# Early K features with the maximum as ScalarE's bias, joined signs, paired sums and a narrower w_out product

## The chip, the cores and the metric

One core of a Trainium2 chip runs the whole kernel. The metric is the device time of one execution in microseconds (us). Names of the engines in the profile: PE is TensorE's matmuls, PEld its weight loads, DVE is VectorE, ACT is ScalarE, POOL is GpSimd, SP the engine that issues all DMAs.

## The reference

```python
proj = x @ w_phi; proj -= max(abs(proj), axis=-1)             # attention features, q and k
phi(x) = concat([exp(proj), exp(-proj)])                      # 256 features per row
kv = phi(k).T @ v;  z = sum_s phi(k)
attn = (phi(q) @ kv) / (phi(q) @ z + 1e-6)                    # B, H, S, D = 8, 8, 576, 64
h = x @ w_in;  g = max(h, 0) + alpha * min(h, 0);  y = g @ w_out     # 4608 tokens, 512 -> 2048 -> 512
logits = y @ phi                                              # soft mixture, 32 slots
slot_in = softmax(logits, over tokens).T @ y;  slot_out = experts(slot_in)
out = softmax(logits, over slots) @ slot_out
```

The weights `w_in` and `w_out` come as 64-bit floats and are converted on the chip.

## The kernel before, in words

`attention_prelu_softmoe` is one program, written as steps. `at(slot, phase, fn)` puts pieces of work into a table of steps, and the loop at its end runs the steps from -45 to 195. A scheduler then sets each engine's own order, from the priorities of this order and from its estimates of durations; each engine runs its instructions in that order, so one that waits holds up all behind it.

- **K pairs** (`k_pair`, 32 of them, two heads each). `project` multiplies K by `w_phi` into the two banks of the one buffer `pk` (pool `ps_b`, shared with the q projections `pq`). `feature` calls `features` for each head: VectorE takes the absolute maximum of 4 x 128 values (L281), subtracts it (L283), and ScalarE writes exp(x) and exp(-x) with one instruction of 512 each (L286, L287). `project_tail` and `feature_tail` do the same for the last 64 rows of two pairs at once. `kv` multiplies the features with V on TensorE (L336) and counts them: pairs 0 to 7 with matmuls on ones (L344), later ones from sums that VectorE makes in `total` (L322, L324), `total_tail` (L328). ScalarE copies the result (L352), `turn` transposes it, and `keep` copies it twice on VectorE (L365, L366). Fourteen pairs come early, the others one per six steps.
- **Weight converts** (`conv`, 16 pieces of `w_in`, then 16 of `w_out`). `first` splits 512 doubles: Abs and Sign on ScalarE (L197, L198), a clamp, a shift, a mask and a scaled product of the low word on VectorE (L199 to L202), a second Abs (L203). `second` adds (L207) and multiplies by the sign (L209). A `w_in` piece is then split in high and low (L222, L223). A `w_out` piece is transposed (L236) and multiplied by `phi`: four matmuls into four groups of 32 rows (L243), a copy (L245), a matmul that adds the groups (L249) and a copy on VectorE (L250).
- **Q pairs** (`q_pair`): the projection (L407), the maximum over partitions on GpSimd (L419, `partition_all_reduce`), the subtraction (L423), two exps (L429), the products with kv and z (L440, L445). For block 0 all of it lies ahead of the first step; `q_finish` takes the reciprocal of the denominator (L462, L463), sends it through DRAM (L465, L470), multiplies (L486) and splits into `xhi`, `xlo` (L479, L480).
- **The first layer** (`gemm`, 12 blocks of 384 tokens, 16 steps each): 12 matmuls per step (L520) into one of two banks `ph`, ScalarE's Relu (L527), VectorE's leaky part (L528). Every step of a block needs `xhi` and `xlo` of the whole block; step c of block 0 needs piece c of `w_in`.

## Time and profile before

| | |
|---|---|
| time, median of 3 runs | 974.15 us (971.86 to 974.99) |
| the profiled execution | 973.75 us, span of its instructions 971.9 us |
| PE busy | 928.3 us, 96% of the span |
| DVE busy | 722.1 us, 74% |
| ACT busy | 443.6 us, 46% |
| POOL busy | 143.5 us, 15% |
| PE busy in 40 slices, tenths | 6888989999989999999999999999999999899997 |
| DVE busy in 40 slices, tenths | 6998999989686687677678778677757767864233 |
| ACT busy in 40 slices, tenths | 5876757766635345245335344353342341221113 |

One slice is 24.3 us. Where PE reads 9 the core is at work on matmuls nearly all the time; the slices below that are the first four, two around 275 us, and the end. In the views, "idle before" is the time an engine stood still ahead of a group of instructions, and "<-" names what it waited for.

### The profile page before, as it was taken

What the parts mean: (1) busy time and instruction counts of PE and PEld (TensorE: products, weight loads), DVE (VectorE), ACT (ScalarE), POOL (GpSimd) and SP (SyncE); (2) the same over time, 40 slices, a digit from 0 to 9 for tenths busy, and PEclk for the clock granted to TensorE, in tenths of its full rate; (3) what the DMA queues carried; (4) which work ended last, traced back from release to release, by engine and by line L of the source; (5) the groups of instructions that cost most, each with busy time, mean ns of one, the idle gap of its engine ahead of it and who ended that gap; (6) DMA issues with size and microseconds to landing.
All of it is one profiled execution on the core that took longest, in us unless ns stands there. A gap on an engine that the chain in (4) does not pass through costs nothing.

```text
span 971.9 us, 20072 instructions
## 1 busy us (share of the span) xinstructions
PE 928.3 (96%) x8178; PEld 654.1 (67%) x8178; DVE 722.1 (74%) x1425; ACT 443.6 (46%) x867; POOL 143.5 (15%) x84
## 2 busy tenths in 40 slices
PE   6888989999989999999999999999999999899997
PEld 3446676777668676676677776776777667786454
DVE  6998999989686687677677778677756767864233
ACT  5876757766635345245335344353342341221113
POOL 4102212112112112122022112121130220000000
PEclk9898999999999999999999999999999999999999
DMA  7345655674231031031211210200212609478999
GB/s 272 119 141 177 207 169 196 213 203 122 64 87 28 23 85 43 26 78 53 51 44 42 59 53 25 75 26 23 54 34 72 177 1 302 159 268 260 311 354 335
DMA packets 75675, 122.22 MB, mean 126 GB/s; under 512 B 7872, under 2 KB 49472, under 8 KB 75584
## 3 DMA queue, kind: packets, MB, share of 16 engines
q1 hardware_dynamic: 75584, 120.95, 40.3%
q8 instruction: 64, 1.05, 0.5%
q14 instruction: 27, 0.22, 0.1%
HBM read 99.82 MB, written 21.10 MB: 124 GB/s over the span
## 4 chain that ended last, share of the span: by engine, by line
PE 74%; DVE 17%; DMA 4%; issue 2%; ACT 2%; SPq 0%; DVEq 0%; ACTq 0%
PE ph L520 37%; PE num L440 5%; PE pkv L336 5%; PE pS L625 4%; PE pl L556 4%; PE pq L407 3%; PE den L445 3%; PE pk L293 2%; PE pso L866 2%; DVE m L207 2%; DVE gT L528 1%; PE pe L846 1%; DVE mx L281 1%; PE po L902 1%; DVE rest L202 1%
## 5 line engine op out<-in xcount | busy, mean ns | idle before, releaser
L520 PE MATMUL ph<-xhi,w 128*128 128x384 f32 x1536 | 430.8, 351 | 8.2 <-ACT xhi L479 4.0
L520 PEld LDWEIGHTS ph<-xhi,w 128*128 128x128 f32 x1536 | 280.3, 189 | 71.5 <-issue 38.0
L520 PE MATMUL ph<-xlo,w 128*128 128x384 f32 x768 | 257.9, 341 | 0.9 <-DVE xlo L480 0.8
L419 POOL PARTITION_ALL_REDUCE mb<-pj x48 | 137.4, 2864 | 477.4 <-ACT pj L413 326.8
L527 ACT ACTIVATE gT<-ph 128x384 f32<-128x384 f32 x192 | 93.3, 488 | 245.3 <-PE ph L520 239.9
L528 DVE SCALAR_TENSOR_TENSOR gT<-gT,alpha_rest,ph 128x384 f32<-128x384 f32 x192 | 115.7, 604 | 103.8 <-ACT gT L527 102.4
L520 PEld LDWEIGHTS ph<-xlo,w 128*128 128x128 f32 x768 | 144.4, 189 | 9.7 <-issue 4.8
L547 DVE STREAM_TRANSPOSE gb<-gT 128x384 f32<-128x384 f32 x162 | 92.0, 571 | 2.9
L429 ACT ACTIVATE qe<-pj 128x768 f32<-128x768 f32 x90 | 72.2, 839 | 22.9 <-DVE pj L423 14.0
L440 PE MATMUL num<-qe,kv 128*64 128x192 f32 (+1 forms) x488 | 68.6, 411 | 3.5 <-ACT qe L429 3.3
L336 PE MATMUL pkv<-kall 128*64 128x256 f32 x464 | 57.9, 393 | 1.3 <-ACT kall L287 0.7
L281 DVE TENSOR_REDUCE mx<-pk 128x4 f32<-128x512 f32 (+1 forms) x80 | 49.5, 623 | 7.2 <-PE pk L293 5.8
L407 PE MATMUL pq<-qraw,wp 64*128 64x384 f32 x192 | 46.8, 545 | 7.9 <-DMA qraw<-in_qT_dram 4.1
L286 ACT ACTIVATE kall<-kall 128x512 f32<-128x512 f32 x60 | 37.5, 627 | 30.4 <-DVE kall L283 30.2
L440 PEld LDWEIGHTS num<-qe,kv 128*64 128x64 f32 x488 | 31.1, 136 | 27.8 <-issue 18.0
L324 DVE TENSOR_TENSOR ks<-ks,kall 128x256 f32<-128x256 f32 x96 | 47.4, 517 | 0.4
L336 PEld LDWEIGHTS pkv<-kall 128*64 128x64 f32 x464 | 31.6, 140 | 23.5 <-issue 4.8
L423 DVE TENSOR_TENSOR pj<-pj,mb 128x768 f32<-128x768 f32 x48 | 44.8, 932 | 0.0
L283 DVE TENSOR_TENSOR kall<-pk,mx 128x512 f32<-128x512 f32 x60 | 40.8, 680 | 2.2 <-PE pkv L336 1.7
L293 PE MATMUL pk<-wp,kall 64*128 64x128 f32 x512 | 39.5, 293 | 2.9 <-issue 2.6
L293 PEld LDWEIGHTS pk<-wp,kall 64*128 64x128 f32 x512 | 32.9, 194 | 12.8 <-issue 10.8
L413 ACT COPY pj<-pq 128x768 f32<-128x768 f32 x44 | 35.0, 796 | 13.4 <-PE pq L407 13.2
(203 smaller groups left out, 1157.6 us busy)
## 6 DMA issues: line engine op xcount, KB each, us to landing
w<-in_w_dram SPq DMA_DIRECT2D x46, 256.0 KB
kall<-in_v_dram SPq DMA_DIRECT2D x30, 320.0 KB
qraw<-in_qT_dram SPq DMA_DIRECT2D x48, 192.0 KB
bc<-rc_d SPq DMA_DIRECT2D x24, 384.0 KB
out_dram<-os SPq DMA_DIRECT2D x18, 512.0 KB
raw<-in_w_in_dram SPq DMA_DIRECT2D x16, 512.0 KB
raw<-in_w_out_dram SPq DMA_DIRECT2D x16, 512.0 KB
gT_d<-gT SPq DMA_DIRECT2D x32, 192.0 KB
```

Source lines behind the costliest of these rows:

```text
L281: nc.vector.tensor_reduce(out=mx[:, 0:nt], in_=src, axis=AX.X, op=ALU.max, apply_absolute_value=True)
L293: lambda t=t, j=j, sl=slice(64 * j, 64 * j + 64): nc.tensor.matmul(st["pk"][:, j, F * t:F * t + F], st["kraw"][sl, 128 * t:128 * t + 128], ...
L324: nc.vector.tensor_tensor(out=ks[:, j], in0=ks[:, j], in1=f[t], op=ALU.add)
L336: return lambda: nc.tensor.matmul(pkv[64 * j:64 * j + 64, 0:256], st["vt"][:, t, 64 * j:64 * j + 64], part.rearrange("p s f -> p (s f)"), ...
L407: lambda j=j, sl=slice(64 * j, 64 * j + 64): nc.tensor.matmul(pq[j][:, 0:BT], wp[sl, F * j:F * j + F], st["qraw"][sl], start=True, stop=True)
L419: nc.gpsimd.partition_all_reduce(mb, pj, 128, bass_isa.ReduceOp.absmax)
L429: nc.scalar.activation(st["e", s], pj, AF.Exp, scale=(1.0, -1.0)[s])
L440: lambda s=s, j=j: nc.tensor.matmul(num[64 * j:64 * j + 64, o:o + w], kvs[:, s, 64 * j:64 * j + 64], st["e", s][:, j, o:o + w], start=(s = ...
L520: gemm_last[0] = nc.tensor.matmul(h, (w_in_hi, w_in_lo)[a][c][:, 128 * k:128 * k + 128], (xhi, xlo)[b][:, k, :], start=(i == 0), stop=(i = ...
L527: nc.scalar.activation(gT, h, AF.Relu, scale=-1.0)
L528: ins = nc.vector.scalar_tensor_tensor(out=gT, in0=gT, scalar=alpha_rest[:, c:c + 1], in1=h, op0=ALU.mult, op1=ALU.add).ins
L547: nc.vector.transpose(out=half_of(n, c // 8)[:, c % 8, :], in_=gT)
```

## The change

- In the first 14 K pairs (`KACT`) VectorE takes one maximum over both heads (8 x 128 values); ScalarE negates it, and reads the projection from PSUM itself, in 8 x 2 exps of 128 values whose bias is that maximum. The subtraction goes. The tails likewise, with 4 exps each.
- In the same 14 pairs the two copies of `keep` go from VectorE to ScalarE.
- In `conv` the sign bit is joined by bit operations on VectorE (a `scalar_tensor_tensor` with AND and OR); ScalarE's Sign and second Abs go, and so does the multiplication by the sign. `rest` has two buffers.
- The sums in `total` cover both heads: three additions of 512 in place of six of 256. The ring of features gives two places at a time.
- The product of `w_out` with `phi` is four matmuls that add up in one set of 32 columns, with `w_out` as the weights; the gathering matmul and one copy go, and the remaining copy is ScalarE's.

```diff
+    def kpair():
+        first = [turns_of["kp"] % KPB, (turns_of["kp"] + 1) % KPB]
+        turns_of["kp"] += 2
+        ring = kall[:, 3200:6272].rearrange("p (n t x) -> p n t x", n=3, t=4)
+        return sorted(first), (0, 1) if first[0] < first[1] else (1, 0), ring
...
-            nc.scalar.activation(m, high, AF.Abs)
-            nc.scalar.activation(sign, high, AF.Sign)
+            nc.scalar.activation(m, high.bitcast(F32), AF.Abs)
             nc.vector.tensor_scalar(out=m, in0=m, scalar1=F64_LEAST, scalar2=F64_MOST, op0=ALU.max, op1=ALU.min)
-            nc.vector.tensor_scalar(out=mu, in0=mu, scalar1=3, scalar2=0x40000000, op0=ALU.logical_shift_left, op1=ALU.bitwise_xor)
-            nc.vector.tensor_scalar(out=ru, in0=mu, scalar1=0x7F800000, scalar2=None, op0=ALU.bitwise_and)
+            nc.vector.tensor_scalar(out=mu, in0=mu, scalar1=3, scalar2=0x3FFFFFFF, op0=ALU.logical_shift_left, op1=ALU.bitwise_and)
+            nc.vector.scalar_tensor_tensor(out=mu, in0=high.bitcast(U32), scalar=0xC0000000, in1=mu, op0=ALU.bitwise_and, op1=ALU.bitwise_or)
+            nc.vector.tensor_scalar(out=ru, in0=mu, scalar1=0xFF800000, scalar2=None, op0=ALU.bitwise_and)
             nc.vector.scalar_tensor_tensor(out=rest, in0=st["low"], scalar=2.0 ** -52, in1=rest, op0=ALU.mult, op1=ALU.mult)
-            nc.scalar.activation(m, m, AF.Abs)
...
-            nc.vector.tensor_tensor(out=m, in0=m, in1=st["rest"], op=ALU.add)
-            mark[slot + 1] = nc.vector.tensor_tensor(out=w, in0=m, in1=st["sign"], op=ALU.mult).ins
+            mark[slot + 1] = nc.vector.tensor_tensor(out=w, in0=st["m"], in1=st["rest"], op=ALU.add).ins
...
                 for k in range(KD):
-                    nc.tensor.matmul(pw[32 * k:32 * k + 32, 0:128], phi_sb[:, k, :], st["wT"][:, 128 * k:128 * k + 128], start=True, stop=True)
-                st["sw"] = prep.tile([128, 128], F32, tag="sw", name="sw")
-                nc.scalar.copy(st["sw"], pw[:, 0:128])
-            def gather():
-                pw = bank("pw2", ps_l)
-                nc.tensor.matmul(pw[:, 0:32], st["sw"], tident[:, 0:32], start=True, stop=True)
-                nc.vector.tensor_copy(wpr[:, c, :], pw[:, 0:32])
+                    nc.tensor.matmul(pw[:, 0:NSL], st["wT"][:, 128 * k:128 * k + 128], phi_sb[:, k, :], start=(k == 0), stop=(k == KD - 1))
+                nc.scalar.copy(wpr[:, c, :], pw[:, 0:NSL])
...
+        def exps(src, dst, nt, mx, nm, read):
+            for t in range(nt):
+                nc.scalar.activation(dst[:, t, 0, :], src[:, t], AF.Exp, bias=nm[:, t:t + 1])
+                ins = nc.scalar.activation(dst[:, t, 1, :], src[:, t], AF.Exp, scale=-1.0, bias=mx[:, t:t + 1]).ins
+            read.append(ins)
+        def most(src, nt):
...
+            nc.vector.tensor_reduce(out=mx, in_=src, axis=AX.X, op=ALU.max, apply_absolute_value=True)
+            nc.scalar.activation(nm, mx, AF.Copy, scale=-1.0)
...
+            if i < KACT:
+                mx, nm = most(st["pk"].rearrange("p j (t f) -> p (j t) f", f=F), 8)
...
+                if i < KACT:
+                    exps(src, kp, 4, mx[:, 4 * j:4 * j + 4], nm[:, 4 * j:4 * j + 4], st["pk_read"])
+                else:
+                    features(src, kp, 4, st["pk_read"])
...
-            for j in range(2):
-                f = [feats(t, j).rearrange("p s f -> p (s f)") for t in range(4)]
-                nc.vector.tensor_tensor(out=ks[:, j], in0=f[0], in1=f[1], op=ALU.add)
-                for t in (2, 3):
-                    nc.vector.tensor_tensor(out=ks[:, j], in0=ks[:, j], in1=f[t], op=ALU.add)
+            f = [st["both"][:, :, t] for t in range(4)]
+            nc.vector.tensor_tensor(out=ks, in0=f[0], in1=f[1], op=ALU.add)
+            for t in (2, 3):
+                nc.vector.tensor_tensor(out=ks, in0=ks, in1=f[t], op=ALU.add)
...
-            nc.vector.tensor_copy(kvs, st["pt"][:, 0:256].rearrange("p (s c) -> p s c", s=2))
-            st["pt_read"].append(nc.vector.tensor_copy(zt[:, :, p], st["pt"][:, 256:384].rearrange("p (g r) -> p g r", g=4)[:, :, 0]).ins)
+            copy = nc.scalar.copy if i < 14 else nc.vector.tensor_copy
+            copy(kvs, st["pt"][:, 0:256].rearrange("p (s c) -> p s c", s=2))
+            st["pt_read"].append(copy(zt[:, :, p], st["pt"][:, 256:384].rearrange("p (g r) -> p g r", g=4)[:, :, 0]).ins)
```

How the instructions stand now. In the changed kernel line 204 is the clamp (L199 before), 205 the shift, 206 the new join of the sign, 207 the mask, 208 the scaled product (L202), 212 the addition, 226 the low part (L223), 284 the new maximum, 486 and 487 the denominator and its reciprocal (L462, L463).

VectorE just ahead of the first reciprocal, before:

```order
L365 COPY kv<-pt 128x256
L366 COPY zt<-pt 128x4
L199 TENSOR_SCALAR m<-m 128x512
L207 TENSOR_TENSOR m<-m,rest 128x512
L200 TENSOR_SCALAR m<-m 128x512
L281 TENSOR_REDUCE mx<-pk_535 128x2
L281 TENSOR_REDUCE mx<-pk 128x4
L209 TENSOR_TENSOR w_813<-m,sign 128x512
L201 TENSOR_SCALAR rest<-m 128x512
L283 TENSOR_TENSOR kp<-pk_535,mx 128x2x128
L462 TENSOR_SCALAR rd<-den 128x192
```

and in the changed kernel:

```order
L206 SCALAR_TENSOR_TENSOR m<-raw,m 128x512
L212 TENSOR_TENSOR w_995<-m,rest 128x512
L284 TENSOR_REDUCE mxa<-pk_591 128x2
L284 TENSOR_REDUCE mxa<-pk 128x8
L207 TENSOR_SCALAR rest<-m 128x512
L486 TENSOR_SCALAR rd<-den 128x192
L226 TENSOR_TENSOR w_997<-w_995,w_997 128x512
L204 TENSOR_SCALAR m<-m 128x512
L208 SCALAR_TENSOR_TENSOR rest<-raw,rest 128x512
L487 RECIPROCAL rd<-rd 128x192
```

The reductions and subtractions of K have given their places to converts. Counted from the first clamp (L199, L204) to the reciprocal, the row before held 8 L199, 8 L200, 8 L201, 8 L202, 7 L207, 7 L209, 7 L223, 10 L281 and 9 L283 of 512, two small ones of each, 4 copies L365, 4 L366 and 3 L423. The row now holds 12 clamps, 11 shifts, 11 joins, 11 masks, 11 scaled products, 10 additions, 10 low parts, 5 maxima of 1024 and two small ones, and 3 subtractions of q.

ScalarE behind block 0's `xhi` (L479 before, L503 now; L551 is the Relu, L527 before), in the changed kernel, first the head of a run of exps:

```order
L389 COPY kv<-pt 128x256
L390 COPY zt<-pt 128x4
L503 CAST xhi<-num 128x384 x4
L285 ACTIVATE nma<-mxa 128x8
L277 ACTIVATE kall<-pk,nma 128x128
L278 ACTIVATE kall<-pk,mxa 128x128
```

and 12 exps of the same pair later its end:

```order
L277 ACTIVATE kall<-pk,nma 128x128
L278 ACTIVATE kall<-pk,mxa 128x128
L375 COPY kvT<-pkv 128x384
L225 CAST w_1114<-w_1112 128x512
L203 ACTIVATE m<-raw 128x512
L551 ACTIVATE gT<-ph 128x384 x2
```

where before it read

```order
L222 CAST w_884<-w_882 128x512
L197 ACTIVATE m<-raw 128x512
L198 ACTIVATE sign<-raw 128x512
L203 ACTIVATE m<-m 128x512
L286 ACTIVATE kall<-kall 128x4x128
L413 COPY pj<-pq 128x768
L287 ACTIVATE kall<-kall 128x4x128
L527 ACTIVATE gT<-ph 128x384 x2
```

The first two Relus of the gemm now stand behind all 16 exps of a K pair, where one exp pair stood. In the first 40 steps ten such pairs follow; most are issued as runs of 8 to 16 exps with no Relu between.

TensorE at a `w_out` piece (L236, now L239, transposes the next one), before:

```order
L243 MATMUL pw<-wT,phi_sb 32x128 x4
L236 MATMUL pwt<-ident,w_1560 128x128 x4
L440 MATMUL num<-qe,kv 64x384 x4
L407 MATMUL pq<-qraw,wp 128x384 x2
L520 MATMUL ph<-xhi,w_615 128x384 x8
L249 MATMUL pw_1734<-tident,sw 128x32
```

and in the changed kernel:

```order
L239 MATMUL pwt<-ident,w_1608 128x128 x4
L469 MATMUL den<-qe,zt 32x192 x8
L431 MATMUL pq<-qraw,wp 128x384 x2
L246 MATMUL pw<-phi_sb,wT 128x32 x4
L464 MATMUL num<-qe,kv 64x384 x4
```

The gathering matmul that came some work later is gone for all sixteen pieces, and the four of each piece have 32 columns and full weights.

## Rows read from the trace of the kernel before

**Rows 1.** Busy time by stretch: opening, early steps (two), saturated steps.

```profile
core 0: us, PE busy (x) PEld busy (x) DVE busy (x) ACT busy (x) POOL busy (x), PEclk, DMA share, GB/s
15.30:63.30 48.00, 40.37 (x438) 22.59 (x438) 47.76 (x89) 40.78 (x76) 9.92 (x3) 0.89 0.43 140
76.60:260.00 183.40, 175.82 (x1426) 133.85 (x1428) 171.47 (x327) 124.72 (x244) 36.83 (x20) 0.99 0.56 172
260.00:280.00 20.00, 17.45 (x159) 10.46 (x156) 16.74 (x36) 10.79 (x21) 0.00 (x0) 0.91 0.23 64
280.00:800.00 520.00, 519.94 (x4415) 370.52 (x4421) 375.28 (x725) 218.93 (x416) 92.59 (x48) 1.00 0.19 52
```

**Rows 2.** Timeline, reciprocal to first gemm: start, length, what [idle before].

```profile
63.30 1.33 DVE L463 RECIPROCAL rd<-rd 128x192 f32<-128x192 f32 x1
75.41 1.50 DVE L486 TENSOR_TENSOR num<-bc,num 128x384 f32<-128x384 f32 x3 [3.36 <-DMA bc<-rc_d]
76.56 0.69 PE L520 MATMUL ph<-xhi,w 128*128 128x384 f32 x1 [3.98 <-ACT xhi L479]
```

**Rows 3.** VectorE's groups by form: xcount | busy us, mean ns | idle before.

```profile
L199 DVE TENSOR_SCALAR m<-m 128x512 f32<-128x512 f32 x32 | 14.4, 454 | 5.1 <-ACT m L197 5.1
L200 DVE TENSOR_SCALAR m<-m 128x512 uint32<-128x512 uint32 x32 | 16.1, 506 | 0.3
L201 DVE TENSOR_SCALAR rest<-m 128x512 uint32<-128x512 uint32 x32 | 17.0, 532 | 0.1
L202 DVE SCALAR_TENSOR_TENSOR rest<-raw,rest 128x512 f32<-128x512 uint32 x32 | 25.7, 805 | 0.3
L207 DVE TENSOR_TENSOR m<-m,rest 128x512 f32<-128x512 f32 x32 | 24.6, 769 | 0.5 <-ACT m L203 0.2
L209 DVE TENSOR_TENSOR w<-m,sign 128x512 f32<-128x512 f32 x32 | 22.0, 690 | 0.8 <-PE pwt L236 0.5
L223 DVE TENSOR_TENSOR w<-w,w 128x512 fp32r<-128x512 f32 x16 | 11.8, 736 | 0.0
L281 DVE TENSOR_REDUCE mx<-pk 128x4 f32<-128x512 f32 x64 | 43.2, 675 | 5.8 <-PE pk L293 5.8
L283 DVE TENSOR_TENSOR kall<-pk,mx 128x512 f32<-128x512 f32 x60 | 40.8, 680 | 2.2 <-PE pkv L336 1.7
L365 DVE COPY kv<-pt 128x256 f32<-128x256 f32 x32 | 13.1, 410 | 11.5 <-PE pt L358 11.2
```

**Rows 4.** ScalarE's groups by form.

```profile
L287 ACT ACTIVATE kall<-kall 128x512 f32<-128x512 f32 x60 | 37.4, 628 | 0.9
L198 ACT ACTIVATE sign<-raw 128x512 f32<-128x512 f32 x32 | 21.5, 673 | 0.0
L245 ACT COPY sw<-pw 128x128 f32<-128x128 f32 x16 | 4.2, 265 | 4.5 <-PE pw L243 4.5
L826 ACT ACTIVATE acc<-px,lsum 128x256 f32<-128x256 f32 x1 | 0.5, 473 | 4.4 <-PE px L821 4.4
```

**Rows 5.** Timeline: two exps of ScalarE back to back.

```profile
149.44 1.17 ACT L287 ACTIVATE kall<-kall 128x512 f32<-128x512 f32 x2
```

**Rows 6.** Timeline of TensorE: the old product, its gathering matmul, four of the new form.

```profile
163.21 0.42 PE L243 MATMUL pw<-wT,phi_sb 128*32 128x128 f32 x8
155.80 0.30 PE L249 MATMUL pw<-tident,sw 128*128 128x32 f32 x2
910.33 0.98 PE L829 MATMUL psi<-tident,acc 128*128 128x32 f32 x8
```

**Rows 7.** Waits of TensorE, 76 to 280 us: total us, times, longest.

```profile
PE num L440 <- ACT qe L429: 3.3, 2, 2.6
PE pkv L342 <- DVE ks L328: 2.4, 1, 2.4
```

**Rows 8.** Chain of waits: start, length of one gemm step's matmuls.

```profile
322.61 2.29 PE ph L520 x12
```

**Rows 9.** Timeline: an all-reduce of GpSimd, and VectorE beside it.

```profile
28.84 4.02 POOL L419 PARTITION_ALL_REDUCE mb<-pj  x1 [4.60 <-ACT pj L411]
30.30 2.04 DVE L202 SCALAR_TENSOR_TENSOR rest<-raw,rest 128x512 f32<-128x512 uint32 x1
```

More of the change, by code (lines that the diff above doesn't have):

```diff
@@ L38 @@
 NDEF = 2
+KACT = 14
 QUADS = [[148, 150, 152, 154], [164, 166, 168, 170]]
@@ L191, in first @@
             pair = st["raw"].rearrange("p (n t) -> p n t", t=2)
[L192 removed]
+            st["low"], high = pair[:, :, 0].bitcast(U32), pair[:, :, 1]
             m = st["m"] = prep.tile([128, 512], F32, tag="m", name="m", bufs=2)
[L194 to L195 removed]
+            rest = st["rest"] = prep.tile([128, 512], F32, tag="rest", name="rest", bufs=2)
             mu, ru = m.bitcast(U32), rest.bitcast(U32)
[L197 to L198 removed]
+            nc.scalar.activation(m, high.bitcast(F32), AF.Abs)
             nc.vector.tensor_scalar(out=m, in0=m, scalar1=F64_LEAST, scalar2=F64_MOST, op0=ALU.max, op1=ALU.min)
[L200 to L201 removed]
+            nc.vector.tensor_scalar(out=mu, in0=mu, scalar1=3, scalar2=0x3FFFFFFF, op0=ALU.logical_shift_left, op1=ALU.bitwise_and)
+            nc.vector.scalar_tensor_tensor(out=mu, in0=high.bitcast(U32), scalar=0xC0000000, in1=mu, op0=ALU.bitwise_and, op1=ALU.bitwise_or)
+            nc.vector.tensor_scalar(out=ru, in0=mu, scalar1=0xFF800000, scalar2=None, op0=ALU.bitwise_and)
             nc.vector.scalar_tensor_tensor(out=rest, in0=st["low"], scalar=2.0 ** -52, in1=rest, op0=ALU.mult, op1=ALU.mult)
[L203 removed]
         def second():
[L206 to L207 removed]
             w = prep.tile([128, 512], F32, tag="w32", name="w32", bufs=2)
[L209 removed]
+            mark[slot + 1] = nc.vector.tensor_tensor(out=w, in0=st["m"], in1=st["rest"], op=ALU.add).ins
             use(slot, w)
@@ L297, in feature @@
         def feature():
-            for j in range(2):
+            if i < KACT:
+                mx, nm = most(st["pk"].rearrange("p j (t f) -> p (j t) f", f=F), 8)
+            order = (0, 1)
+            if i not in (1, 3):
+                at2, order, ring = kpair()
+                a, b = at2
+                st["both"] = ring[:, a:b + 1:b - a]
+            for j in order:
                 if i in (1, 3):
@@ L301, in feature @@
                 else:
[L302 removed]
+                    kp = ring[:, at2[j]].rearrange("p t (s f) -> p t s f", s=2)
                 st["kp", j] = kp
[L304 removed]
+                src = st["pk"][:, j].rearrange("p (t f) -> p t f", f=F)
+                if i < KACT:
+                    exps(src, kp, 4, mx[:, 4 * j:4 * j + 4], nm[:, 4 * j:4 * j + 4], st["pk_read"])
+                else:
+                    features(src, kp, 4, st["pk_read"])
         def project_tail():
@@ L312, in feature_tail @@
             kp = tail_k[i // 2] = attk.tile([128, 2, 2, F], F32, tag="kp1", name="kp")
-            features(st["pk4"][:, 0:2 * F].rearrange("p (t f) -> p t f", f=F), kp, 2, st["pk4_read"])
+            src = st["pk4"][:, 0:2 * F].rearrange("p (t f) -> p t f", f=F)
+            if i < KACT:
+                exps(src, kp, 2, *most(src, 2), st["pk4_read"])
+            else:
+                features(src, kp, 2, st["pk4_read"])
         def feats(t, j):
@@ L319, in total @@
             ks = st["ks"] = attk.tile([128, 2, 2 * F], F32, tag="ks", name="ks")
-            for j in range(2):
-                f = [feats(t, j).rearrange("p s f -> p (s f)") for t in range(4)]
-                nc.vector.tensor_tensor(out=ks[:, j], in0=f[0], in1=f[1], op=ALU.add)
-                for t in (2, 3):
-                    nc.vector.tensor_tensor(out=ks[:, j], in0=ks[:, j], in1=f[t], op=ALU.add)
+            f = [st["both"][:, :, t] for t in range(4)]
+            nc.vector.tensor_tensor(out=ks, in0=f[0], in1=f[1], op=ALU.add)
+            for t in (2, 3):
+                nc.vector.tensor_tensor(out=ks, in0=ks, in1=f[t], op=ALU.add)
         def total_tail():
```

10 lines of the change are left out of this document (3 added, 7 removed).

## The prediction

> **What bounds the kernel now.** I read the busy time by stretch first, then the timeline where a stretch ends, then the groups of instructions for prices. From 280 to 800 us TensorE is busy 519.94 of 520 us [rows 1]: nothing that VectorE or ScalarE saves there can shorten it, and VectorE has 375 of 520 us there, a share of 72%. What can be won lies before. The opening, from the first convert to the first reciprocal (15.3 to 63.3 us), is VectorE's: busy 47.76 of 48.00 us, ScalarE 40.78, TensorE 40.37 [rows 1]. The reciprocal at 63.30 us goes out through DRAM, comes back for the divisions at 75.41, and the first gemm starts at 76.56, after TensorE stood still for 3.98 us [rows 2]. From there to 280 us TensorE is busy 175.82 + 17.45 of 203.4 us [rows 1], so it loses 10.1 us, and the lower granted clock between 260 and 280 us (0.91) costs another 0.09 x 20 = 1.8. The two largest waits there, 3.3 us for `qe` behind a late subtraction and 2.4 us for a late sum [rows 7], are VectorE's lateness, directly or at one remove. So there are two places to win: an earlier first gemm, and at most 11.9 us in the early steps.
>
> **The change, opening.** The change takes work from VectorE, but the order of the changed kernel does not put the reciprocal earlier in that work: more converts stand ahead of it. With the counts given with the change and the means of [rows 3], the row of instructions ahead of the reciprocal gains 4 clamps (4 x 0.454 = 1.8 us), 3 shifts (1.5), 3 masks (1.6), 3 scaled products (2.4), 3 additions (2.3), 3 low parts (2.2), 11 joins and 5 maxima of 1024. A join reads two tensors of 512, one of them with every second word, like L202; VectorE's forms bound it by 0.69 (L209) and 0.805 (L202), and I take 0.75: 8.2 us. A maximum of 1024 cannot take more than two of 512 (1.35) nor less than one (0.675); most of its length goes by elements, so I take 1.2: 6.0. Sum added 26.0. It loses 7 multiplications by the sign (7 x 0.69 = 4.8), 10 maxima of 512 (6.8), 9 subtractions (6.1), 2 small ones (at half of 0.68, 0.7) and four pairs of copies (4 x 0.41 and four shorter, some 2.2). Sum lost 20.6. The counts of both are nearly the same, so what neighbours overlap drops out. Net **+5.4 us** on an engine that had 0.24 us to spare in 48. The reciprocal, the DRAM trip and the first gemm all come that much later. Bounds: +3 if joins and maxima cost their least (11 x 0.06 and 5 x 0.3), +9 if ScalarE makes VectorE wait as well.
>
> Does ScalarE? The row for a 128-wide exp with a bias from memory does not exist. From below it is the 128-wide copy from PSUM, 0.265 us; a 256-wide one with a scale from memory took 0.473, where 128 and 512 (0.265, 0.628) put a plain one at 0.39 [rows 4], so the pointer adds 0.09 and one exp is some 0.35. Two neighbours took 1.17 where each alone is 0.628 [rows 4, 5], an overlap of 0.09. I take a step of 0.27, between 0.18 (no pointer cost) and 0.35 (no overlap). In the opening ScalarE gets 72 of them in place of 17 exps of 512 and 4 of 256: +19.4 - 10.7 - 1.7; it loses 9 Signs and 7 second Abs (at 0.67 and 0.63: -10.4) and gains 3 more converts (two instructions each, +4.0) and 4 pairs of copies and 5 negations (+3.3). Net +3.9: 44.7 of 53.4 us. So it is not the bound unless the step exceeds 0.27 + 8.7/72 = 0.39.
>
> **The change, early steps.** VectorE's load between 76.6 and 280 us is 188.2 us of 203.4 [rows 1], 93%. It loses the other 19 subtractions (12.9), ten pairs of copies (5.5), three converts that are now done earlier (13) and smaller sums: some 31 us, which leaves 77%. At 72% in the steps after 280 us TensorE loses nothing, so most of the 11.9 us should come back. I take **-8**, and leave 4 for ScalarE's longer runs of exps. Bounds 0 and -12.
>
> **The change, `w_out` product.** On TensorE a piece took 0.42 + 0.30 us; the four matmuls at L829 have the new form exactly and took 0.98 [rows 6]. That is +0.26 x 16 = +4.2 us, in a stretch that TensorE bounds, if none of it lies beside neighbours. It can also be a gain: one block and one hand-over through ScalarE fewer per piece, up to -0.30 x 16 = -4.8 if the weights load beside other matmuls. I take **+2**: the same-form row is the nearest, and half of its excess is start-up that neighbours share.
>
> **Costed at nothing:** the paired sums, which save VectorE three starts per pair, are covered after 280 us by a TensorE without idle time; if that cover went they would be a gain, not a loss. Moving `wpr`'s copy to ScalarE is hidden by a ScalarE at 61% (124.7 + 10.8 of 203.4 [rows 1]). The DMA queue keeps its issues; the loads of converts come earlier with them.
>
> Sum: +5.4 - 8 + 2 = -0.6. The profiled execution took 973.75 us (span 971.9, so 1.85 around it), 0.4 below the median of 974.15. Forecast **973 us**, no change that a measurement can tell: runs of this kernel tell about 0.3%, 2.9 us, from none.
>
> **Weighing a rule.** Beside an all-reduce of GpSimd a scaled product took 2.04 us against its mean of 0.805 [rows 3, 9]; three all-reduces lie in the opening, 9.92 us together [rows 1]. The Trainium skill (SBUF — State Buffer, Who interferes with whom) says that VectorE and GpSimd share one pair of SBUF ports by an exclusive lock, that a VectorE instruction in a two-port mode or with two SBUF inputs waits out the other, and that reductions never do. The trace agrees for the scaled product. By that rule the change is worse than its sum: it removes the maxima and subtractions, which read PSUM, and leaves converts that can be blocked. That is the third rival below.
>
> **Rivals.**
> - *Faster.* The opening grows by the least (+3), the product costs nothing, and all of the 11.9 us comes back: 973.75 + 3 - 11 = 966. For it: VectorE had the blame for the waits in [rows 7], and TensorE without a gap is what the trace shows at 72% load. Against: the opening's +5.4 is a plain count on a full engine. Chance 0.34.
> - *Slower: Relus behind exps.* In the early steps ten runs of up to 16 exps, 16 x 0.27 = 4.3 us, stand ahead of Relus. `ph` has two banks and a step's matmuls take 2.29 us [rows 8], so a Relu held for a whole run stops TensorE for about 2 us unless it has K or q work at hand. Five of ten such stops are +10: 973 + 10 = 983. It decides against me from the second such stop on, when the 4 us that I leave are used up. For it: the order behind block 0's `xhi`. Against: half of TensorE's instructions in this stretch are not gemm. Chance 0.20.
> - *Slower: the blocked opening.* If in the changed kernel every all-reduce of the opening stops VectorE for its whole length, 9.92 us, where one third (2.04 - 0.8 per long stop, some 3 us) is paid now, the opening grows by 7 more: 980. For it [rows 9]; against, VectorE's queue is in order, so it already stopped there. Chance 0.10.
> - *The change doesn't do what it says*: the runs of exps hold `pk`'s only buffer longer, so a K projection comes later; it has been priced with the first slower rival.
>
> **How the numbers follow.** The forecast's own case, 968 to 978, has 0.36. Faster by over 0.3% is the first rival, 0.34; the two slower ones together 0.30. The range reaches to 963 (the faster rival with a product that gains) and to 984 (the Relu rival), leaving out some 0.2.
>
> **What would show it.** Right: the first reciprocal near 69 us and the first gemm near 82; VectorE still busy over 95% in the opening; TensorE's idle time from the first gemm to 280 us down from 10 to some 3 us; L246's four matmuls 0.8 to 1.0 us; exps near 0.35 us each, 0.27 apart. Wrong: a first gemm before 78 us (the count ahead of the reciprocal did not bind); waits of L520 for the leaky part above 5 us (Relu rival); exps over 0.39 us apart; converts above 1.5 us at every all-reduce (blocked opening).

## The result, and the profile after

The changed kernel takes 979.26 us (median of 4 runs, 978.48 to 981.79) where the kernel before, run beside it on the same chip, takes 973.3 (971.86 to 974.99): a ratio of 1.0065, 95% interval 1.0039 to 1.0092. It is slower by 6 us, inside the range that was given, but not the "no change" that was forecast. The profiled execution took 979.78 us, its span is 978.0.

Busy time of the changed kernel by engine, from the page:

```profile
PE 937.0 (96%) x8146; PEld 660.9 (68%) x8146; DVE 689.5 (71%) x1260; ACT 447.5 (46%) x1034; POOL 144.7 (15%) x84
```

VectorE lost 33 us of work, as intended, and ScalarE gained 4. TensorE, which sets the end, has 32 matmuls fewer and is busy 8.7 us longer. The same stretches as in [rows 1], of the changed kernel:

```profile
15.30:63.30 48.00, 37.44 (x410) 21.49 (x410) 46.84 (x77) 41.87 (x125) 9.20 (x3) 0.89 0.50 166
76.60:260.00 183.40, 175.65 (x1430) 134.59 (x1429) 141.52 (x231) 119.78 (x326) 39.54 (x20) 0.99 0.56 171
260.00:280.00 20.00, 20.00 (x149) 15.29 (x149) 14.81 (x25) 9.03 (x19) 0.00 (x0) 1.00 0.09 24
280.00:800.00 520.00, 519.93 (x4328) 367.28 (x4324) 368.47 (x661) 219.32 (x412) 91.81 (x48) 1.00 0.20 54
```

The opening is still VectorE's (46.84 of 48.00 us), and between 76.6 and 260 us VectorE fell from 171.47 to 141.52 us. The steps that answer to [rows 2]:

```profile
68.84 1.34 DVE L487 RECIPROCAL rd<-rd 128x192 f32<-128x192 f32 x1
82.41 1.96 DVE L510 TENSOR_TENSOR num<-bc,num 128x384 f32<-128x384 f32 x4 [6.02 <-DMA bc<-rc_d]
83.56 1.85 PE L544 MATMUL ph<-xhi,w 128*128 128x384 f32 x7 [1.18 <-ACT xhi L503]
```

The reciprocal is 5.54 us later, the divisions 7.00, the first gemm 7.00. To see where the 6 us lie, I divided both profiled executions at the same work: from the first matmul to the first gemm, from there to the start of the 57th gemm step, which lies behind the early steps, and from there to the last matmul. Stretch, length, then busy time and count of TensorE, its weight loads, VectorE, ScalarE and GpSimd, and the granted clock. Before:

```profile
4.00:76.50 72.50, 55.45 (x605) 32.01 (x605) 62.82 (x116) 51.22 (x96) 12.66 (x4) 0.91 0.57 184
76.60:344.10 267.50, 257.37 (x2142) 192.74 (x2143) 232.75 (x449) 161.21 (x312) 48.83 (x28) 0.99 0.44 133
344.10:965.60 621.50, 615.41 (x5432) 429.29 (x5431) 423.85 (x845) 229.74 (x460) 80.59 (x40) 1.00 0.37 114
```

After:

```profile
4.00:83.50 79.50, 60.86 (x605) 34.19 (x605) 63.66 (x107) 58.99 (x180) 11.94 (x4) 0.89 0.60 191
83.60:349.40 265.80, 259.23 (x2110) 196.98 (x2111) 201.68 (x338) 155.94 (x395) 51.31 (x28) 1.00 0.41 126
349.40:972.00 622.60, 616.78 (x5433) 429.58 (x5431) 421.51 (x800) 231.17 (x460) 80.03 (x40) 1.00 0.38 115
```

The opening is 7.0 us longer, the early steps 1.7 shorter, the rest 1.1 longer: +6.4. In the opening the same 605 matmuls take TensorE 5.4 us more busy time, at a lower clock, and it idles 1.6 us more (18.64 against 17.05, length less busy time). In the early steps its idle time fell from 10.13 to 6.57 us, and its busy time rose by 1.9.

What TensorE waited for in the opening is new (total us, times, longest):

```profile
PE pk L302 <- ACT kp L278: 7.2, 2, 5.5
PE pq L431 <- DMA qraw<-in_qT_dram: 3.9, 1, 3.9
PE pk L302 <- ACT kall L278: 3.5, 2, 2.4
PE pkv L359 <- ACT kp L278: 3.4, 2, 1.9
PE pkv L359 <- ACT kall L278: 1.6, 1, 1.6
```

Four of the five rows name the exps of the K features (L278), 15.7 us together; the fifth, for q's first load, lies for the most part ahead of the first matmul and stood before too. In the opening of before the K exps had 2.8 us of TensorE's waits. The 15.7 us are not a price by themselves: other waits of before went, 3.7 us of the q projections and 2.2 of the transposes among them, and all idle time of TensorE in the opening rose by only the 1.6 us above. The longest wait stands where a run of exps holds `pk`. ScalarE's timeline there, and TensorE's behind it:

```profile
25.64 0.37 ACT L277 ACTIVATE kp<-pk,nma 128x128 f32<-128x128 f32 x1
25.90 0.37 ACT L278 ACTIVATE kp<-pk,mxa 128x128 f32<-128x128 f32 x1
26.15 0.38 ACT L277 ACTIVATE kp<-pk,nma 128x128 f32<-128x128 f32 x1
...
29.15 0.48 ACT L277 ACTIVATE kp<-pk,nma 128x128 f32<-128x128 f32 x1
29.40 0.49 ACT L278 ACTIVATE kp<-pk,mxa 128x128 f32<-128x128 f32 x1
```

```profile
29.94 2.08 PE L302 MATMUL pk<-wp,kall 64*128 64x128 f32 x16 [5.48 <-ACT kp L278]
```

The sixteen exps are 0.25 us apart, 4.25 us from the first start to the last end, and the next projection starts 0.05 us after the last of them. Until then TensorE stood still for 5.48 us.

### The profile page after: what moved, and what is told of

Read it like the earlier page. It is cut to its first block, busy times and chain, and to the rows that moved or that the text cites. A ratio compares the mean times of both kernels' runs of the same rounds, so it can differ in the third digit from the quotient of the medians.

```text
span 978.0 us, 19983 instructions
## 1 busy us (share of the span) xinstructions
PE 937.0 (96%) x8146; PEld 660.9 (68%) x8146; DVE 689.5 (71%) x1260; ACT 447.5 (46%) x1034; POOL 144.7 (15%) x84
## 4 chain that ended last, share of the span: by engine, by line
PE 81%; DVE 8%; ACT 6%; DMA 3%; issue 1%; SPq 0%; DVEq 0%; ACTq 0%
PE ph L544 40%; PE num L464 6%; PE pkv L359 6%; PE pS L649 4%; PE pl L580 4%; PE pq L431 3%; PE den L469 3%; PE pk L302 3%; PE pso L890 2%; PE pw L246 1%; PE pe L870 1%; PE po L926 1%; DMA bc<-rc_d 1%; ACT kall L277 1%; PE pt L381 1%
## 5 line engine op out<-in xcount | busy, mean ns | idle before, releaser
L551 ACT ACTIVATE gT<-ph 128x384 f32<-128x384 f32 x192 | 95.0, 500 | 256.9 <-PE ph L544 251.2
L359 PE MATMUL pkv<-kall 128*64 128x256 f32 x464 | 61.4, 403 | 3.4 <-ACT kp L278 1.9
L302 PE MATMUL pk<-wp,kall 64*128 64x128 f32 x512 | 41.6, 301 | 11.9 <-ACT kp L278 7.2
L469 PE MATMUL den<-qe,zt 128*32 128x192 f32 x720 | 40.5, 332 | 0.0
L649 PE MATMUL pS<-gb,d 32*32 32x512 f32 (+1 forms) x1056 | 40.3, 579 | 0.0
L278 ACT ACTIVATE kall<-pk,mxa 128x128 f32<-128x128 f32 x96 | 40.3, 419 | 0.0
L277 ACT ACTIVATE kall<-pk,nma 128x128 f32<-128x128 f32 x96 | 39.6, 412 | 0.6 <-PE pkv L367 0.3
```

The costliest lines, as they stand in the source:

```text
L302: lambda t=t, j=j, sl=slice(64 * j, 64 * j + 64): nc.tensor.matmul(st["pk"][:, j, F * t:F * t + F], st["kraw"][sl, 128 * t:128 * t + 128], ...
L359: return lambda: nc.tensor.matmul(pkv[64 * j:64 * j + 64, 0:256], st["vt"][:, t, 64 * j:64 * j + 64], part.rearrange("p s f -> p (s f)"), ...
L469: lambda s=s, j=j, h=h, zt=kv_t[NP * ((n * BT + h * HB) // S) + p][1]: nc.tensor.matmul(den[64 * j + 32 * h:64 * j + 32 * h + 32, 0:HB], z ...
L551: nc.scalar.activation(gT, h, AF.Relu, scale=-1.0)
L649: ins = nc.tensor.matmul(pS[i][32 * (j % 4):32 * (j % 4) + 32, width * h:width * h + width], st["d"][32 * i:32 * i + 32, 32 * j:32 * j + 3 ...
```

## The experiments

Every ratio is to the kernel before, run beside it on the same chip; its median was 972.3 to 973.7 us throughout. What is read from a profile is one execution of a kernel, the times are medians of several.

**First theories.** Theory 1: the new product's extra work on TensorE, and an opening made longer by the converts that now stand ahead of the reciprocal. Theory 2: ScalarE's runs of exps are the whole loss.

### The old product put back in the changed kernel

```diff
-                    nc.tensor.matmul(pw[:, 0:NSL], st["wT"][:, 128 * k:128 * k + 128], phi_sb[:, k, :], start=(k == 0), stop=(k == KD - 1))
-                nc.scalar.copy(wpr[:, c, :], pw[:, 0:NSL])
+                    nc.tensor.matmul(pw[32 * k:32 * k + 32, 0:128], phi_sb[:, k, :], st["wT"][:, 128 * k:128 * k + 128], start=True, stop=True)
+                st["sw"] = prep.tile([128, 128], F32, tag="sw", name="sw")
+                nc.scalar.copy(st["sw"], pw[:, 0:128])
...
+            at(slot + 4, "pe", gather)
```

> The changed kernel with the old w_out product (four matmuls into four groups of rows, copy, gathering matmul, VectorE's copy). Theory 1 (TensorE pays for the new product: its 16 sets took 13.97 us to the next instruction, the old ones 5.88 + 4.11 with one 0.8 us wait in it): 979.3 - 4.5, some 975; the first gemm stays near 83.6. Theory 2 (ScalarE's runs of exps are the whole loss): the product changes nothing, 979.

Measured: 985.44 us, 1.0110 (1.0086 to 1.0134). Both theories missed, on the same side: without the part that was to cost TensorE time the kernel is no faster, and by its median slower still (the two intervals touch).

### The new product alone, in the kernel before

> The kernel before with the new w_out product alone. Theory 1: 973.3 + 4.5, some 978, with the first gemm still near 76.6. Theory 2: 973, since nothing else of the change is in it.

Measured: 972.64 us, 0.9991 (0.9981 to 1.0001). The edit is the one above the other way round. Here it costs nothing, though TensorE is busy longer on it: 16.52 us, much as in the changed kernel (16.32, below), against 12.03. TensorE's idle time over the three stretches fell by about as much, from 33 to 29 us, nearly all of it in the early steps, which are as long as before (267.9 us against 267.5): in this order the added work lies where TensorE waited before. The profiled execution, 976.64 us, is the slowest of the twelve; its opening is 3.8 us longer than the one of before.

### The converts held behind the reciprocal

```diff
+            if slot >= HELD:
+                tc.add_manual_dep(ins, mark["recip"].name, nosync, reason="behind the reciprocal")
```

> The changed kernel, with the converts of w_in from the ninth on held behind block 0's reciprocal on VectorE by an order without a wait. Theory 1 (converts ahead of the reciprocal make the first gemm late): reciprocal near 63, first gemm near 77 to 78, the total down by 5 to 6, some 973.5. Theory 2 (the opening is ScalarE's): the reciprocal stays within 2 us of 68.8 because the features of the last K pair come no earlier, and the total stays at 977 to 979. A third possibility: the held converts come too late for the steps of block 0 and the waits of the gemm give the gain back, 976 to 979 with an early first gemm.

> Both edits: converts held behind the reciprocal and the old product. Theory 1: the two prices are independent, 979.3 - 5.5 - 4.5, some 969, below the kernel before. Theory 2: 977 to 979.

Measured: 983.64 us, 1.0107 (1.0087 to 1.0127), and with the old product 982.84, 1.0093 (1.0072 to 1.0114). The first gemm came at 77.4 and 77.1 us, 6 us earlier than in the changed kernel, and the end 4 us later: every case of the two expectations missed the time. The first of the two, in the second stretch of [rows 1]:

```profile
76.60:260.00 183.40, 171.35 (x1324) 132.91 (x1325) 148.80 (x245) 116.22 (x317) 36.56 (x19) 0.96 0.54 170
```

TensorE has 1324 matmuls done there in place of 1430, at a clock of 0.96. The converts that were moved out of the opening are done here, where VectorE has 148.80 us of work in place of 141.52. None of TensorE's waits there names a convert; the two largest are 4.7 us for the exps of K and 3.2 us for the leaky part. So the time of the first gemm, on which the prediction's opening term rests, isn't a price by itself.

Nor is VectorE's count of work the only thing that holds the reciprocal. From the first clamp to the reciprocal, in the changed kernel and with the converts held:

```profile
15.63:68.84 53.21, 40.78 (x445) 23.14 (x446) 52.38 (x87) 45.34 (x136) 9.20 (x3) 0.90 0.48 158
15.50:64.63 49.13, 37.82 (x432) 21.52 (x428) 42.75 (x67) 42.10 (x128) 9.68 (x3) 0.87 0.45 146
```

VectorE has 9.6 us less to do, 5.0 less even than in the kernel before, but the reciprocal comes only 4.2 us earlier, still behind the 63.30 us of before. VectorE now stands idle for 6.4 us of the stretch, while TensorE's waits for the exps of K are still 14.0 us.

**Second theories.** Theory 3: the K part is the loss. Theory 4: any edit puts the engines' shared order another way, and that costs, whatever the edit is.

### Each part alone, or all but one

The K part alone, in the kernel before (`exps` and `most` as in the change, for the tails too):

```diff
-                features(st["pk"][:, j].rearrange("p (t f) -> p t f", f=F), kp, 4, st["pk_read"])
+                src = st["pk"][:, j].rearrange("p (t f) -> p t f", f=F)
+                if i < KACT:
+                    exps(src, kp, 4, mx[:, 4 * j:4 * j + 4], nm[:, 4 * j:4 * j + 4], st["pk_read"])
...
+            copy = nc.scalar.copy if i < 14 else nc.vector.tensor_copy
```

> The kernel before with the K part alone: maximum as bias of ScalarE's exps for K pairs 0 to 13, and their keep copies on ScalarE. Theory 3 (the K part is the loss: TensorE waits in the opening for runs of 16 exps that hold the two PSUM banks of pk): 979 to 984, with waits of pk, pkv for the exps of 12 to 17 us before the first gemm. Theory 4 (no part costs by itself; each edit only puts the shared order of the work another way and the loss is spread over the early steps): 970 to 976 here, no more than e_sign is off.

The changed kernel without its K part:

```diff
-KACT = 14
+KACT = 0
...
-            copy = nc.scalar.copy if i < 14 else nc.vector.tensor_copy
+            copy = nc.vector.tensor_copy
```

> The changed kernel without its K part: K features as before (VectorE subtraction, two long exps), keep copies on VectorE; joined sign, paired sums and the new w_out product stay. Theory 3: 968 to 973, no slower than before, since the exps from PSUM are gone; reciprocal 62 to 64 us. Theory 4: 977 to 984, since the three other edits put the order another way as well.

The joined sign alone, with the second buffer of `rest`, in the kernel before:

```diff
-            nc.scalar.activation(sign, high, AF.Sign)
...
+            nc.vector.scalar_tensor_tensor(out=mu, in0=high.bitcast(U32), scalar=0xC0000000, in1=mu, op0=ALU.bitwise_and, op1=ALU.bitwise_or)
...
-            nc.scalar.activation(m, m, AF.Abs)
```

> The kernel before with the joined sign alone. It takes two 0.7 us ScalarE passes from each of the 32 converts and leaves VectorE's work nearly as it was. Theory 3: 970 to 974. Theory 4: 976 to 984, the loss of the whole change being as likely to show here as anywhere.

The changed kernel with the keep copies alone put back:

```diff
-            copy = nc.scalar.copy if i < 14 else nc.vector.tensor_copy
+            copy = nc.vector.tensor_copy
```

> The changed kernel with the keep copies of K pairs 0 to 13 back on VectorE (2 copies of 0.25 to 0.45 us each). Theory 3, if the exps are the loss: 978 to 981 as the changed kernel. If instead the copies are the loss, because they queue on ScalarE behind runs of 16 exps and the gemm of the pair's values waits for them: 972 to 975, and fewer waits of TensorE before 300 us. Theory 4: anywhere from 974 to 985.

The paired sums alone, in the kernel before, with `kpair` for the places. They were run with the next group, where theory 5 is that the parts cost of themselves, whatever the order:

```diff
+            f = [st["both"][:, :, t] for t in range(4)]
+            nc.vector.tensor_tensor(out=ks, in0=f[0], in1=f[1], op=ALU.add)
+            for t in (2, 3):
+                nc.vector.tensor_tensor(out=ks, in0=ks, in1=f[t], op=ALU.add)
```

> The kernel before with the paired sums alone (three additions of 512 columns in place of six of 256 for K pairs 8 and up, and features written into pairs of ring places). Theory 5: 971 to 974, since VectorE has 47 us of these additions and less of them now. Theory 4: 975 to 985; the joined sign alone gave 4 us more, the K part alone 12 us more.

| kernel | us | ratio (95%) | first gemm |
|---|---|---|---|
| K part alone | 984.86 | 1.0131 (1.0110 to 1.0152) | 73.8 |
| all but the K part | 980.99 | 1.0084 (1.0063 to 1.0106) | 78.2 |
| sign alone | 976.99 | 1.0042 (1.0025 to 1.0058) | 79.1 |
| all, keep on VectorE | 983.43 | 1.0107 (1.0090 to 1.0124) | 83.5 |
| sums alone | 977.76 | 1.0054 (1.0034 to 1.0074) | 76.5 |

The parts alone add up to 12 + 4 + 5 - 1 = 20 us, the whole change costs 6. Taking the keep copies off ScalarE makes the change 4 us slower, not faster (the intervals just touch); with the K part out it is no faster either, and the intervals overlap. For the K part alone theory 4 missed by far, and theory 3 by 0.9 us; its sign did not come, since TensorE's waits for the exps ahead of the first gemm were 6.5 us and not 12 to 17. For the next three theory 3 missed, the case of the dear copies too, and theory 4 held; for the sums theory 5 missed and theory 4 held. Prices that don't add speak for theory 4, and the next runs put it to the test against theory 5.

### The same instructions in another order

Three reorderings of the kernel before, each two independent lines exchanged, nothing added or removed: Sign ahead of Abs, head 1's features ahead of head 0's, the two copies of `keep`. The last of them:

```diff
-            nc.vector.tensor_copy(kvs, st["pt"][:, 0:256].rearrange("p (s c) -> p s c", s=2))
-            st["pt_read"].append(nc.vector.tensor_copy(zt[:, :, p], st["pt"][:, 256:384].rearrange("p (g r) -> p g r", g=4)[:, :, 0]).ins)
+            nc.vector.tensor_copy(zt[:, :, p], st["pt"][:, 256:384].rearrange("p (g r) -> p g r", g=4)[:, :, 0])
+            st["pt_read"].append(nc.vector.tensor_copy(kvs, st["pt"][:, 0:256].rearrange("p (s c) -> p s c", s=2)).ins)
```

Sign first, and heads:

```diff
-            nc.scalar.activation(m, high, AF.Abs)
             nc.scalar.activation(sign, high, AF.Sign)
+            nc.scalar.activation(m, high, AF.Abs)
```

```diff
-            for j in range(2):
+            for j in (1, 0):
```

> The kernel before, with nothing changed but the order in which two independent ScalarE passes of a convert are written (Sign ahead of Abs): the same instructions of the same sizes, put in another order on every engine. Theory 4 (any edit that moves the shared order off the one of before costs, whatever it adds or removes): 975 to 985. Theory 5 (the parts themselves cost: more work on an engine or a bank held longer, and not the order): 971 to 975, as before.

> The kernel before, with the K features of head 1 written ahead of those of head 0: the same instructions in another order. Theory 4: 975 to 985. Theory 5: 971 to 975.

> The kernel before, with the two VectorE copies that keep a K pair's sums written in the other order: the same instructions in another order. Theory 4: 975 to 985. Theory 5: 971 to 975. If the three reorderings lie within 0.3% of before and of each other, the order is no cause and the parts' own prices have to carry the sum.

And three of the changed kernel: heads, the two copies (exchanged as above), and the two exps of each 128 columns.

```diff
-            for j in order:
+            for j in order[::-1]:
```

```diff
-                nc.scalar.activation(dst[:, t, 0, :], src[:, t], AF.Exp, bias=nm[:, t:t + 1])
-                ins = nc.scalar.activation(dst[:, t, 1, :], src[:, t], AF.Exp, scale=-1.0, bias=mx[:, t:t + 1]).ins
+                nc.scalar.activation(dst[:, t, 1, :], src[:, t], AF.Exp, scale=-1.0, bias=mx[:, t:t + 1])
+                ins = nc.scalar.activation(dst[:, t, 0, :], src[:, t], AF.Exp, bias=nm[:, t:t + 1]).ins
```

> The changed kernel, with the K features of its two heads written in the other order: the same instructions. Theory 4 (order alone; the parts are worth nothing): between 972 and 980, as the kernels before with a reordering. Theory 5 (the parts cost 6 us of themselves, the order comes on top): 979 to 986.

> The changed kernel, with the two copies that keep a K pair's sums written in the other order: the same instructions. Theory 4: between 972 and 980. Theory 5: 979 to 986.

> The changed kernel, with the two exps of each 128 columns written in the other order (the one that needs no negated maximum first): the same instructions. Theory 4: between 972 and 980. Theory 5: 979 to 986.

| order | kernel before, us | ratio (95%) | changed kernel, us | ratio (95%) | first gemm, before / changed |
|---|---|---|---|---|---|
| as written | 972 to 974 | 1 | 979.26 | 1.0065 (1.0039 to 1.0092) | 76.6 / 83.6 |
| Sign first | 974.08 | 1.0015 (1.0004 to 1.0027) | - | - | 78.9 / - |
| heads | 975.77 | 1.0036 (1.0021 to 1.0051) | 995.57 | 1.0220 (1.0194 to 1.0246) | 76.6 / 89.8 |
| keep copies | 979.42 | 1.0069 (1.0053 to 1.0084) | 983.78 | 1.0113 (1.0099 to 1.0126) | 76.1 / 80.3 |
| exps | - | - | 985.60 | 1.0130 (1.0116 to 1.0144) | - / 89.7 |

Theory 5 held for the first reordering, theory 4 for the other two: order alone, with the same instructions, costs the kernel before up to 6.7 us, as much as the whole change. But theory 4 in its pure form falls too: the changed kernel's three reorderings lie at 984 to 996, above the whole band of 972 to 980 that was given for it, and theory 5 held for two of them. The mean ratio of the four orders is 1.0030 before and 1.0132 after: averaged so, what the change computes costs some 10 us, and as written it came out in the cheapest of its four orders. Four orders of each are few, and they aren't the same four.

In the dearest order of the kernel before, that of the keep copies, the trace shows where the time went. The products of K's features with V on TensorE (`pkv`), ahead of the first gemm and from there to the 57th step, as written:

```profile
4.00:76.50 72.50, 26.08 (x360) 0.91 0.57 184
76.60:344.10 267.50, 32.71 (x372) 0.99 0.44 133
```

and with the copies exchanged:

```profile
4.00:76.00 72.00, 22.84 (x300) 0.96 0.57 185
76.10:351.30 275.20, 38.42 (x432) 0.99 0.42 128
```

Sixty of them run behind the first gemm instead of ahead of it, in a stretch that TensorE bounds: that stretch is 7.7 us longer, 5.7 of it in these matmuls. The first gemm itself comes no later. In the K part alone the same sixty stay behind, beside an early first gemm; in no other order of this section do they.

The two dearest orders of the changed kernel have a common mark. The heads order in the first stretch of [rows 1], and TensorE's waits up to 75 us:

```profile
15.30:63.30 48.00, 33.04 (x355) 19.08 (x354) 45.96 (x75) 37.97 (x112) 9.92 (x3) 0.79 0.43 152
```

```profile
PE pk L302 <- ACT kp L278: 9.0, 2, 6.5
...
PE pkv L359 <- ACT kp L278: 2.6, 3, 1.5
```

TensorE gets 355 matmuls done in those 48 us in place of 410, the granted clock is 0.79 in place of 0.89, the longest wait for `pk` is 6.5 us where it was 5.5. The reciprocal comes at 75.9. The exps order waits 10.5 us for the same line, 7.9 the longest, and has its reciprocal at 75.8. The waits are not all of it: VectorE also has more work ahead of the reciprocal, 57.33 us in the heads order where it was 52.38, since yet more of the converts stand there.

### The product twice, and the exps out of the opening

```diff
+                for k in range(KD):
+                    nc.tensor.matmul(pw[:, NSL:2 * NSL], st["wT"][:, 128 * k:128 * k + 128], phi_sb[:, k, :], start=(k == 0), stop=(k == KD - 1))
```

> The changed kernel with the new w_out product made twice (a second time into unused columns of its bank): 64 more products of 0.22 us, 14 us more work for TensorE. If TensorE's work sets the end: 990 to 995 (14 us more than 979, less 0 to 3 where it falls into a wait). If the product falls into waits, as the product alone seemed to (973): 979 to 984.

As the first case had it: 993.19 us, 1.0210 (1.0196 to 1.0224), 14 us above the changed kernel. TensorE on `pw` from 150 to 275 us, in the kernel before, the changed kernel, and this one:

```profile
150.00:275.00 125.00, 12.03 (x160) 1.00 0.50 149
```

```profile
150.00:275.00 125.00, 16.32 (x128) 15.99 (x128) 3.56 (x16) 1.00 0.48 146
```

```profile
150.00:275.00 125.00, 30.82 (x256) 30.22 (x256) 3.29 (x16) 1.00 0.44 136
```

The second 14.5 us stand in the end time almost whole. In the changed kernel little idle time is left to take more work (6.6 us in the early steps); in the kernel before, with 10.1, there was room for 4 us.

```diff
-            if i < KACT:
+            if 6 <= i < KACT:
...
-            copy = nc.scalar.copy if i < 14 else nc.vector.tensor_copy
+            copy = nc.scalar.copy if 6 <= i < 14 else nc.vector.tensor_copy
```

> The changed kernel with K pairs 0 to 5, whose work lies ahead of the first gemm, made as in the kernel before, and only pairs 6 to 13 by exps from PSUM. If the exps cost in the opening alone and help behind it: 970 to 976, first gemm at 76 to 80 us. If they cost as much later (ScalarE's runs of exps ahead of the gemms' Relus): 979 to 985. If only the order speaks: anywhere from 974 to 985.

The heads order of the changed kernel, with `KACT = 0` and the keep copies on VectorE:

> m_heads (996) without the K part: K features and keep copies as in the kernel before; joined sign, paired sums, new product and the reordered heads stay. If the exps from PSUM in the opening make the orders dear: 976 to 984, first gemm at 76 to 80 us. If the product's work and the order alone do: 988 to 996.

Measured: the changed kernel with the exps from pair 6 on, 976.53 us, 1.0041 (1.0026 to 1.0056), half a microsecond above the first band; first gemm at 77.3 us, idle time of TensorE in the early steps 5.5 us. The heads order without the K part: 983.33 us, 1.0111 (1.0092 to 1.0129), inside the band of its first case; first gemm at 75.1. Its opening:

```profile
15.30:63.30 48.00, 41.73 (x440) 24.07 (x440) 47.86 (x89) 31.71 (x59) 9.21 (x3) 0.86 0.41 141
```

440 matmuls in place of 355, VectorE at 47.86 us in place of 45.96, the first gemm 14.7 us earlier, and 12 us off the end. So the K part is what makes that order dear, and it does so ahead of the first gemm. That it is the exps' hold of `pk`, and not the rest of the K part or the order that comes with it, is read from the waits and not shown: no run gave `pk` a second buffer. With pairs 0 to 5 spared, the change as written gains 2.7 us; the two intervals touch, so that alone would not settle it. Behind the opening the exps may even help (976.5 with them, 981.0 without any), but 4.5 us is no more than an order moves, and this stays open. No version here beats the kernel before; the new product alone is level with it.

## Why the prediction was wrong

**The step that failed.** The sum came out 7.0 us too low, and no single term carries that: each of its terms erred towards the faster side, the product most. And one wait, that for `pk` behind a run of exps, stood in it at nothing.

**The opening, +5.4.** Right for the order it was given, and nearly in size: VectorE stayed full (52.38 of 53.21 us), the reciprocal came 5.54 us later. The row prices held: a join 0.68 us (0.75 taken), a maximum of 1024 1.21 (1.2 taken), exps 0.37 us at first and 0.25 apart (0.35 and 0.27). The lower bound of +3 took 0.3 us off each maximum, where the prediction's own least of 0.675 takes off 0.5: it should have been +2. The first gemm moved 7.0, since the trip through DRAM took 13.6 us from reciprocal to division where it took 12.1; that was not priced.

**The early steps, -8.** -1.7 was measured with the product inside; set its +4.3 aside and -6.0 is left, 3.6 of it idle time; the other 2.4 go with a granted clock of 1.00 in place of 0.99 over 267 us, which isn't shown to be the whole of it. In place of "from 10 to some 3" the idle time fell to 6.6.

**The product, +2.** This is a term that was mis-sized: 16.32 - 12.03 = +4.3 us of TensorE time, just past the upper bound of +4.2, which was the plain row of the same form [rows 6]. The half that was taken off as start-up "that neighbours share" was not there: even counted to the next instruction the sixteen sets take 13.97 us against 9.99, 4.0 more. Doubling the product showed that this stretch forgives hardly anything more.

**Behind the early steps, nothing was forecast**, and +1.1 came. "TensorE has no idle time" [rows 1] isn't "the same matmuls take the same time": where a set of them is cut by others, it takes longer. The clearest case lies shortly ahead of the 57th step, inside the early steps, a set of 96 small matmuls of the later sums. Before:

```profile
332.06 3.41 PE L625 MATMUL pS<-gb,d 32*32 32x512 f32 x96
335.40 0.44 PE L520 MATMUL ph<-xlo,w 128*128 128x384 f32 x1
```

and after, cut by gemm matmuls behind its second:

```profile
336.39 1.04 PE L649 MATMUL pS<-gb,d 32*32 32x512 f32 x2
337.36 0.44 PE L544 MATMUL ph<-xlo,w 128*128 128x384 f32 x1
...
338.61 3.39 PE L649 MATMUL pS<-gb,d 32*32 32x512 f32 x94
341.93 0.44 PE L544 MATMUL ph<-xlo,w 128*128 128x384 f32 x1
```

From its start to the next instruction the whole set takes 3.34 us, the cut one 0.97 + 3.32. That is 0.95 us of the early steps. Behind the 57th step these sums take about as long as before (41.67 us of busy time against 41.24). There it is the products with V, 420 matmuls in either kernel, before and after:

```profile
344.10:965.60 621.50, 42.47 (x420) 1.00 0.37 114
349.40:972.00 622.60, 44.05 (x420) 1.00 0.38 115
```

Some of their sets of 20 are cut after the second in the changed kernel, and together they are busy 1.6 us longer. Whether that is the whole of the +1.1 isn't shown.

The sum with the measured sizes is 7.0 - 6.0 + 4.3 + 1.1 = +6.4, against -0.6 as forecast: 1.6 from the opening, 2.0 from the early steps, 2.3 from the product, 1.1 from behind, 7.0 in all. These are the sizes in one execution of one order; an order alone moved the time by as much, and putting the old product back gained nothing, so none of them is a price that can be had back by itself. "About 0.3%" as what the runs can tell took in only how executions of one kernel differ, and not that.

**The rivals.** *Faster* needed +3 from the opening and all of the early steps' idle time back, and got +7.0 and a third of it; its free product cost 4.3. *Relus behind exps* did not come: TensorE's waits for the leaky part in the early steps were 2.7 us, below the 5 that were to decide. *The blocked opening* showed its sign, but not its price: at each of the three all-reduces a convert on VectorE now took over 1.5 us, where before it was at two of them. Against the plain lengths of the same instructions that is some 1 us more than before, and not 7.

```profile
16.09 1.92 DVE L205 TENSOR_SCALAR m<-m 128x512 uint32<-128x512 uint32 x1
18.05 0.69 DVE L206 SCALAR_TENSOR_TENSOR m<-raw,m 128x512 uint32<-128x512 uint32 x1
...
21.05 2.15 DVE L212 TENSOR_TENSOR w<-m,rest 128x512 f32<-128x512 f32 x1
...
31.17 2.16 DVE L212 TENSOR_TENSOR w<-m,rest 128x512 f32<-128x512 f32 x1
```

By the rule of the Trainium skill (SBUF — State Buffer, Who interferes with whom) a VectorE instruction with two inputs in SBUF, like L212, contends with GpSimd, and a reduction never does. The trace agrees in part: in the kernel before, a maximum at 22.17 us, beside the all-reduce of 21.27 to 24.25, took its plain 0.68 us, but in the changed kernel L206, with two inputs in SBUF, took its plain 0.69 us at 18.05, while the all-reduce of 16.06 to 18.98 still ran. *That the runs of exps hold `pk`* was named last, "priced with the first slower rival", and so put at no cost in the opening. That is the step that failed in kind: ScalarE was asked whether it had time in all (44.7 of 53.4 us; it had, 45.67 of 53.54), not who stands still while a run of 16 lasts. What the runs show in its place: TensorE waits 15.7 us for the exps there; making the first six pairs as before gains 2.7 us as written, by intervals that touch, while taking the whole K part out gains 12 in the heads order and nothing in the order as written (980.99 us). How much of the 6 us this wait alone costs stays open.

## What to carry to other kernels

When an engine that has time to spare takes over reading a buffer that exists once, price how long the buffer is held and who waits for it, not the engine's load. A saving or a cost on the engine that sets the end counts against the idle time that is left there: 4 us disappeared in a kernel with 10 us of early idle time, 14 came through nearly whole where there were 7. When an order moves the time, count which instructions of the engine that sets the end have changed sides of its last long wait: sixty matmuls that did were 5.7 us here. And where a scheduler sets the order, exchange two independent lines of the kernel before first: if that moves the time as far as the edit does, one measurement of the edit doesn't tell what the edit is worth.

## What the runs showed of the hardware that was not expected

TensorE can run at about half speed where the clock column of a view reads 1.00. In the kernel before, two projections of a q pair, and in its reordering with the copies exchanged, the same two:

```profile
20.08 0.91 PE L407 MATMUL pq<-qraw,wp 64*128 64x384 f32 x2
```

```profile
16.16 1.64 PE L407 MATMUL pq<-qraw,wp 64*128 64x384 f32 x2 [0.79 <-ACT pj L411]
17.74 3.68 PE L336 MATMUL pkv<-kall 128*64 128x256 f32 x16
21.35 1.65 PE L407 MATMUL pq<-qraw,wp 64*128 64x384 f32 x2
```

The stretch around the first of them, with its granted clock in the third place from the end:

```profile
4.00:20.00 16.00, 13.65 (x58) 7.70 (x60) 9.04 (x12) 7.93 (x16) 5.66 (x2) 1.00 0.87 308
```

0.91 us there, 1.64 here, with a granted clock of 1.00 written. All profiled executions begin so: the first matmuls take 1.7 to 1.8 times as long as later equals, near the ratio of the two levels, 2.4 and 1.2 GHz. The trace has no clock record for that time, and the column counts such time as full clock: the first record lies at 9.5 us in the kernel before, at 19.1 in the changed kernel and at 29.7 in this reordering. So part of the 5.4 us by which TensorE is busier in the changed kernel's opening is this start. Compare the lengths of equal matmuls in an opening, not the clock column alone. What sets the length of that start was not tried, and each kernel has one profile.

ScalarE's 128-wide exps with a bias from memory come 0.25 us apart whatever their written length, which grows from 0.37 to 0.49 us within a run of sixteen. Their pitch is the price; their sum isn't.
